# Down products in two operations, and a new order of every engine's work, in a kernel of attention and a gated two-layer product

## The chip, the cores and the metric

The kernel runs on one core of one Trainium2 chip. The metric is the time of one execution in microseconds (us) of device time, lower is better, given as the median of several runs. Beside the runs stands one profiled execution, whose trace gives each engine's instructions and waits.

Engines are called as the profile calls them: PE is TensorE (its products; PEld its weight loads), DVE is VectorE, ACT is ScalarE, POOL is GpSimd, SP is SyncE, whose queue issues every transfer here.

## The reference

Blocked attention with a local window and block summaries over 4 batches, 8 heads, 768 positions and 64 columns of a head, then two matrix products with a gate between, over 3072 tokens of 512 columns and 2048 inner columns:

```python
k_sum = k.reshape(B, H, nb, block, D).max(axis=3)      # nb = 24 blocks of 32
v_sum = v.reshape(B, H, nb, block, D).mean(axis=3)
scores_l = scale * q @ k.T          # where |row - column| < 16, else -1e9
scores_s = scale * q @ k_sum.T + log(block)
a = softmax(concat(scores_l, scores_s))
x = a @ concat(v, v_sum)            # laid out as 3072 x 512
h = x @ w_in                        # w_in 512 x 2048, w_out 2048 x 512
out = (h * cos(h)) @ w_out
```

Inputs q, k and v are float32; the two weight matrices come as float64.

## The kernel before, in words

The tokens are worked in eight blocks of 384 (half a batch each). In each block attention runs in four groups of two heads, called a, b, c and d with the block's number: a0 is the first group of block 0. The two products run in 128 **steps** s0 to s127, one for each block and each of 16 slices of 128 inner columns; block 0 is worked in two parts (slices 0 to 5, then 6 to 15), with block 1 between.

A **step** is this chain (class Step): *up*, 12 products on PE of 128x128 by 128x384 into one PSUM bank (line 707); *turns* on ACT (717), *residue* on DVE (720), *sine* and *square* on ACT (725, 728), *gate* on DVE (732), which together make h * cos(h) with the sign turned; *high part*, the gate's result rounded to a narrower float32 form (a copy, on ACT line 343 or on DVE line 345); *low part*, what the rounding left (a subtraction, line 349, on POOL or DVE); *down*, 9 products of 128x128 by 128x512 into three banks that stay open for all steps of a block (line 754). The products are made exact enough by splitting both sides in high and low: up multiplies x high by w_in high, x low by w_in high and x high by w_in low; down multiplies, for each of three chunks of 128 tokens, gate high by w_out high, gate high by w_out low and gate low by w_out high, in this order. The tiles t, gh and gl of the chain have two buffers each (pool gp), so step n + 2 writes what step n read.

A **group** loads q, k and v, turns q and k (on PE with an identity matrix, lines 495 and 508, or on DVE in squares of 32), makes *scores* (48 small products on 64 rows and 64 columns of PE, line 562) into two banks, *scales* them out of the banks (573, or a copy), subtracts the maximum (POOL), takes the exponential (ACT, line 599, with a table load when the table changes), divides by the sum (POOL), turns the result (*tp* with its copies *cp*, line 619, or through DRAM) and multiplies it with the values (*va*, 24 products on 120 rows and 64 columns, line 663) into one bank, from which x high and x low are taken (343 or 345, 349).

The float64 **weights** w0 to w15 are loaded a slice at a time, 1 MB each in two transfers (lines 364 and 368), and turned into a high and a low float32 part by integer operations: *magnitude* on ACT (line 381), four operations on DVE (386, 392, 400, 408), *high part* (343 or 345) and *low part* (349). The sums of v by blocks (v0_0 and so on) are made on DVE and POOL and spread to the groups by small transfers (line 486).

What sets the order: one table, ORDER, a string of words written out ahead. Each word names who (s5, a2, w3), what (up, hi, dn, and so on), the PSUM banks, and the engine where there is a choice (a for ACT, v for DVE, p for POOL). A loop at the end of the kernel goes through it and issues each word's instructions; every engine keeps that order, and so does SP's queue of transfers. Semaphores make an instruction wait for what it needs; behind a waiting instruction everything later on its engine waits too. Eight PSUM banks are shared by all: three hold the open sums of down, the other five go round among ups, turns, scores and values.

Of the kernel before, what the change touches and what calls it, by code (L numbers as in the profile page):

```python
# [32 lines left out]
d0.sc c0.su w1.lb a0.tp.0.0 w0.ab.1 a0.tp.1.4 d1.q w1.fb.0 a0.cp.0.a w2.l a0.cp.1.a w0.cl d0.z.1.a w1.hi.a w5.l
w0.sh.0.1 a0.va.5 d0.z.0.a b0.m w1.lo.p w0.lb c0.ex d0.m a0.xh.a d0.mx c0.sm d0.su w3.l c0.iv w2.ab.1 a0.xl c0.nm
w0.fb.0 d0.ex b0.v c0.tp.0.6 w2.cl w0.hi.a d0.sm c0.tp.1.7 c0.cp.0.a w0.lo.p c0.m w2.sh.2.3 c0.cp.1.a w2.lb w5.ab.1
c1.q w2.fb.0 a1.q d0.iv w2.hi.a w5.cl d0.nm d0.v w5.sh.4.5 c0.va.0 w4.l w5.lb w3.ab.1 w2.lo.p d1.m d0.tp.0.1 c0.xh.a
b0.mx d0.tp.1.6 c0.xl d0.cp.0.a b0.su a1.tq.7 b1.q w5.fb.0 d0.cp.1.a d0.va.2 a1.cq.a a1.m b0.ex w3.cl a1.ms.3.0
w5.hi.a w3.sh.6.7 d1.v a1.sc d0.xh.a w5.lo.p b0.sm w4.ab.1 c1.tq.1 c1.v c1.ms.4.5 w3.lb a1.z.1.a a1.z.0.a b1.tq.0
b0.iv b1.m w4.cl b0.nm c1.cq.a b1.cq.a a1.mx c1.sc c1.m w4.sh.0.1 c1.z.1.a a1.su b0.tp.0.3 c1.z.0.a b0.tp.1.5 d0.xl
a1.v b0.cp.0.a w4.lb b1.ms.4.2 b0.cp.1.a a1.ex w8.l c1.mx b0.va.3 b1.v a1.sm b1.sc c1.su b0.xh.a b0.xl d1.tq.5  # L40
b1.z.1.a a1.iv s0.up.3 a2.q w4.fb.0 a1.nm c1.ex b1.z.0.a b2.v c1.sm w4.hi.a d1.ms.2.0 c1.iv w3.fb.1 s0.tu c1.nm
d1.cq.a a1.tp.0.1 w7.l w4.lo.v s1.up.4 w3.hi.a w9.l a1.cp.0.a w3.lo.p b1.mx w8.ab.0 w6.l d1.sc s0.re s1.tu w8.cl
a1.tp.1.5 v1_0.l s2.up.6 d1.z.0.a w10.l b1.su d1.z.1.a s1.re a1.cp.1.a s0.si d1.mx a1.va.7 w8.sh.0.1 d1.su a2.tq.2
a2.v c1.tp.0.5 s0.sq w8.lb s1.si s1.sq c1.cp.0.a s0.ga s1.ga c1.tp.1.5 s0.hi.a w8.fb.1 s1.hi.a s0.lo.p c1.cp.1.a
w9.ab.0 s0.dn.3.4.5 s1.lo.p w8.hi.v b2.q s2.tu d1.ex s2.re w8.lo.p a2.cq.v a1.xh.v s3.up.0 a1.xl s2.si d1.sm v1_0.s.p
d1.iv w9.cl c1.va.1 s2.sq d1.nm v1_1.l s3.tu s1.dn c1.xh.a s3.re w7.ab.1 c1.xl s2.ga s2.hi.a w7.cl s4.up.2 s3.si
s2.lo.p w9.sh.6.7 s3.sq b1.ex v1_1.s.p s3.ga d1.tp.0.1 w9.lb d1.tp.1.0 s2.dn s4.tu b1.sm v1_2.l d1.cp.1.a d1.cp.0.a
s4.re s5.up.0 s3.hi.a b1.iv w9.fb.0 b1.nm s4.si w9.hi.v s3.lo.p d1.va.1 w7.sh.6.7 s4.sq d1.xh.a w9.lo.p s3.dn s5.tu
w7.lb w10.ab.1 s5.re s4.ga s5.si v1_2.s.p d1.xl s4.hi.a b1.tp.0.2 w7.fb.0 s5.sq b1.tp.1.1 b1.cp.0.a b1.cp.1.a s4.lo.p
s5.ga w12.l w7.hi.a b1.va.2 s5.hi.v v1_3.l s4.dn w10.cl s5.lo.p b1.xh.a b1.xl w7.lo.p w10.sh.6.7 s6.up.1 w6.ab.1  # L50
w10.lb w10.fb.0 s7.up.0 s6.tu v1_3.s.p s6.re w10.hi.a w6.cl s5.dn s7.tu s6.si w10.lo.p v1_4.l s6.sq b2.m s7.re s8.up.2
s5.ta.0.a s6.ga s5.ta.1.v s6.hi.a s5.st.0 s5.ta.2.a w6.sh.6.7 s5.st.1 s6.lo.p w12.ab.0 s5.st.2 a2.m w6.lb v1_4.s.p
s6.dn.1.3.4 s8.tu s7.si s8.re s7.sq w12.cl s8.si v1_5.l s9.up.5 s8.sq s7.ga s8.ga s7.hi.a w6.fb.1 s8.hi.a s7.lo.p
s7.dn s9.tu s8.lo.p w12.sh.6.7 w11.l w6.hi.a s9.re w6.lo.p w12.lb s9.si s10.up.0 s9.sq s9.ga w12.fb.0 s9.hi.a s8.dn
s10.tu s9.lo.p s10.re w12.hi.a w15.l v1_5.s.v w11.ab.1 w12.lo.p s11.up.2 v1_6.l s10.si w11.cl s10.sq s9.dn s11.tu
s11.re s10.ga s11.si w11.sh.6.7 s10.hi.a s12.up.5 s11.sq s10.lo.p w15.ab.0 w11.lb v1_6.s.p s10.dn s12.tu s11.ga s12.re
s11.hi.a w11.fb.1 s12.si s11.lo.p v1_7.l s13.up.0 s12.sq s12.ga w11.hi.a w13.l w15.cl s12.hi.a w15.sh.6.7 s11.dn
s13.tu s12.lo.p s13.re w11.lo.p w15.lb s13.si s12.dn s13.sq s13.ga w15.fb.0 s13.hi.a s13.lo.p s14.up.2 w13.ab.1
w15.hi.v w13.cl w15.lo.p s13.dn s14.tu v1_7.s.v s14.re a2.k s15.up.5 w13.sh.6.7 s14.si s14.sq s14.ga w13.lb s14.hi.a
s16.up.0 s15.tu s14.lo.p s15.re w13.fb.0 s15.si s14.dn s15.sq s16.tu s15.ga w14.l w13.hi.a s16.re a2.tk.0.2 s15.hi.a  # L60
w13.lo.p a2.tk.1.6 a2.ks.0 a2.ck.0.a s17.up.7 b2.k a2.ck.1.a a2.ks.1 s16.si s16.sq s15.lo.p a2.sc.5.2 s16.ga s16.hi.a
s15.dn s17.tu a2.z.1.v s16.lo.p s17.re w14.ab.1 a2.z.0.v a2.mx s17.si s16.dn s17.sq w14.cl a2.su s17.ga s17.hi.a
w14.sh.6.7 b2.tk.0.0 s18.up.2 b2.ck.0.a s17.lo.p a2.ex w14.lb s17.dn w14.fb.0 s18.tu a2.sm w14.hi.a b2.tk.1.5 s18.re
b2.tq.6 w14.lo.p b2.ck.1.a c2.k s19.up.7 b2.ks.1 s18.si b2.ks.0 c2.q b2.cq.v a2.iv b2.sc.5.0 a2.nm s18.sq s19.tu
s18.ga s20.up.6 s19.re s18.hi.a b2.z.0.v s19.si s18.lo.p b2.z.1.v s19.sq b2.mx a2.tp.0.2 s20.tu a2.tp.1.5 c2.tq.0
a2.cp.0.a s19.ga b2.su s18.dn d2.q c2.cq.v a2.cp.1.a s19.hi.a s20.re b2.ex s19.lo.p c2.tk.0.7 c2.tk.1.2 c2.ks.0 s19.dn
d2.k c2.ks.1 c2.ck.0.a b2.sm c2.ck.1.a s20.si b2.iv s21.up.5 b2.nm s20.sq s20.ga s22.up.0 s21.tu s20.hi.a s21.re
# [850 lines left out]
```

## Time and profile before

| | |
|---|---|
| median of 3 runs | 678.76 us (675.94 to 678.94) |
| profiled execution, its own time | 681.43 us |
| its span, first to last instruction | 679.6 us |
| busy on PE, DVE, ACT, POOL | 645.0, 391.0, 411.4, 294.2 us |
| granted clock of PE, mean | 0.98 |
| up: 1536 products, down: 1152 products | 37% and 38% of the chain that ended last |
| scores, values on that chain | 4% and 4% |

Busy time of PE counts pipelined products, whose modelled lengths overlap, so it says less than the chain of waits, which goes back from the last instruction to what released each. In a row of the chain stand start, length and what ran; in a row of the waits who waited for whom, then the total, the number of times and the longest.

### The profile page before, as it was taken

Reading aid. Unit: us, or ns where it says so; the run is one execution under the profiler, and the core shown is the slowest. Engines: PE = TensorE matmul, PEld = TensorE weight load, DVE = VectorE, ACT = ScalarE, POOL = GpSimd, SP = SyncE. Lnnn points to the kernel's source line nnn. Section 1 sums busy time; section 2 is a strip of 40 time slices with the busy share of each in tenths; the row PEclk is TensorE's granted clock in tenths of the full one; section 3 lists DMA queues with packets and bytes.
Section 4 is the critical chain, followed back from the end, with each engine's and each line's share of the span. In section 5 each row is a group of like instructions: output and inputs, shape, how many; then the busy total and the mean of one; then the engine's idle time right before and its main releaser. Section 6 shows DMA issues by size and latency. Waiting matters only on the chain.

```text
span 679.6 us, 13400 instructions
## 1 busy us (share of the span) xinstructions
PE 645.0 (95%) x5180; PEld 567.2 (83%) x5180; DVE 391.0 (58%) x642; ACT 411.4 (61%) x720; POOL 294.2 (43%) x312
## 2 busy tenths in 40 slices
PE   6449889999999999999999999999999999999997
PEld 5337668988889888889888888898988889899996
DVE  4888688988552367435875764347584663223221
ACT  3566787758775458646666666447666575455443
POOL 3656588646252355432443653424353352222221
PEclk9859889999999999999999999999999999999999
DMA  9896924532232224434454463334254341001001
GB/s 222 251 245 165 295 53 164 191 101 52 64 89 56 81 63 117 117 91 103 89 145 115 94 193 97 88 50 103 80 131 106 76 133 52 23 0 47 1 0 47
DMA packets 158543, 71.17 MB, mean 105 GB/s; under 512 B 129552, under 2 KB 147344, under 8 KB 158480
## 3 DMA queue, kind: packets, MB, share of 16 engines
q1 hardware_dynamic: 158480, 70.32, 39.4%
q8 instruction: 41, 0.67, 0.4%
q14 instruction: 22, 0.18, 0.1%
HBM read 52.99 MB, written 14.94 MB: 100 GB/s over the span
## 4 chain that ended last, share of the span: by engine, by line
PE 84%; DMA 6%; DVE 3%; ACT 2%; POOL 2%; issue 1%; SPq 1%; ACTq 0%; POOLq 0%
PE banks L754 38%; PE banks L707 37%; PE banks L562 4%; PE banks L663 4%; DMA late<-in_moe_w_out_dram 3%; DMA vn<-vs 1%; PE banks L508 1%; DMA vn<-in_v_dram 1%; DMA x<-vs 1%; SPq L486 1%; DVE stage L408 1%; ACT stage L381 0%; POOL late L252 0%; PE banks L619 0%; DVE stage L386 0%
## 5 line engine op out<-in xcount | busy, mean ns | idle before, releaser
L707 PE MATMUL banks<-xh,w 128*128 128x384 f32 x1024 | 282.1, 339 | 0.0
L754 PE MATMUL banks<-w,gh 128*128 128x512 f32 x768 | 244.6, 400 | 0.0
L349 POOL TENSOR_TENSOR gl<-t,gh 128x384 fp32r<-128x384 f32 x123 | 126.0, 1025 | 252.0 <-ACT gh L343 184.9
L707 PEld LDWEIGHTS banks<-xh,w 128*128 128x128 f32 x1024 | 187.2, 188 | 4.8 <-DVE xl L349 0.2
L707 PE MATMUL banks<-xl,w 128*128 128x384 f32 x512 | 171.9, 336 | 0.0
L754 PEld LDWEIGHTS banks<-w,gh 128*128 128x128 f32 x768 | 141.3, 189 | 26.3 <-ACT gh L343 0.5
L754 PE MATMUL banks<-w,gl 128*128 128x512 f32 x384 | 152.7, 398 | 0.8 <-POOL gl L349 0.8
L720 DVE SCALAR_TENSOR_TENSOR t<-t,banks 128x384 f32<-128x384 int32 x128 | 70.3, 549 | 130.3 <-ACT t L717 130.1
L717 ACT ACTIVATE t<-banks 128x384 int32<-128x384 f32 x128 | 62.3, 487 | 104.4 <-PE banks L707 102.7
L732 DVE SCALAR_TENSOR_TENSOR t<-t,banks 128x384 f32<-128x384 f32 x128 | 70.2, 549 | 75.5 <-ACT t L728 75.0
L707 PEld LDWEIGHTS banks<-xl,w 128*128 128x128 f32 x512 | 96.3, 188 | 3.9
L725 ACT ACTIVATE t<-t 128x384 f32<-128x384 f32 x128 | 67.1, 524 | 45.0 <-DVE t L720 44.7
L343 ACT CAST gh<-t 128x384 fp32r<-128x384 f32 x115 | 58.8, 512 | 55.1 <-DVE t L732 50.6
L754 PEld LDWEIGHTS banks<-w,gl 128*128 128x128 f32 x384 | 72.8, 190 | 17.9 <-POOL gl L349 2.1
L728 ACT ACTIVATE t<-t 128x384 f32<-128x384 f32 x128 | 67.2, 525 | 3.7
L586 POOL TENSOR_TENSOR sc<-sc,m 128x720 f32<-128x720 f32 x28 | 40.2, 1437 | 41.7 <-DVE m L581 40.4
L610 POOL TENSOR_TENSOR sc<-sc,r 128x720 f32<-128x720 f32 x28 | 39.1, 1401 | 37.7 <-DVE r L607 35.2
L349 POOL TENSOR_TENSOR w<-stage,w 128x1024 fp32r<-128x1024 f32 x15 | 36.1, 2404 | 16.7 <-ACT w L343 16.0
L562 PEld LDWEIGHTS banks<-kd,qd 64*64 64x64 f32 x1344 | 27.5, 132 | 7.9 <-issue 4.8
L602 DVE TENSOR_REDUCE r<-sc 128x6 f32<-128x726 f32 x28 | 25.2, 902 | 14.2 <-ACT sc L599 14.1
L725 ACT ACT_TABLE_LOAD x24 | 30.8, 1283 | 0.4
L381 ACT ACTIVATE stage<-late 128x1024 f32<-128x1024 f32 x16 | 18.4, 1147 | 20.5 <-DMA late<-in_moe_w_out_dram 18.2
(98 smaller groups left out, 588.8 us busy)
## 6 DMA issues: line engine op xcount, KB each, us to landing
late<-in_moe_w_in_dram SPq DMA_DIRECT2D x16, 512.0 KB
late<-in_moe_w_out_dram SPq DMA_DIRECT2D x16, 512.0 KB
pd<-stage SPq DMA_DIRECT2D x20, 384.0 KB
vn<-in_v_dram SPq DMA_DIRECT2D x52, 120.0 KB
out_dram<-stage SPq DMA_DIRECT2D x23, 256.0 KB
pt<-pd SPq DMA_DIRECT2D x60, 96.0 KB
kn<-in_v_dram SPq DMA_DIRECT2D x24, 192.0 KB
qn<-in_q_dram SPq DMA_DIRECT2D x80, 48.0 KB
```

The lines of the kernel that those rows point to most:

```text
L343: eng.copy(out=out, in_=in_)
L349: eng.tensor_tensor(out=lo, in0=src, in1=hi.bitcast(F32), op=ALU.subtract)
L562: nc.tensor.matmul(out=self.sp[hh][s * QT : (s + 1) * QT, c, lo : lo + n], lhsT=self.qd[rows, t * QT : (t + 1) * QT], rhs=self.kd[rows, ke ...
L586: nc.gpsimd.tensor_tensor(out=self.sc, in0=self.sc, in1=self.m.unsqueeze(2).broadcast_to([P, U, NK]), op=ALU.subtract)
L610: nc.gpsimd.tensor_tensor(out=self.sc, in0=self.sc, in1=self.r.unsqueeze(2).broadcast_to([P, U, NK]), op=ALU.mult)
L707: nc.tensor.matmul(out=self.h, lhsT=w_of(name, self.f)[:, c * P : (c + 1) * P], rhs=x_of(self.blk, part, c), start=n == 0, stop=n == last,)
L717: nc.scalar.activation(out=self.t.bitcast(I32), in_=self.h, func=AF.Copy, scale=1.0 / TWO_PI)
L720: nc.vector.scalar_tensor_tensor(out=self.t, in0=self.t.bitcast(I32), scalar=-TWO_PI, in1=self.h, op0=ALU.mult, op1=ALU.add)
L725: nc.scalar.activation(out=self.t, in_=self.t, func=AF.Sin, scale=0.5)
L728: nc.scalar.activation(out=self.t, in_=self.t, func=AF.Square, scale=math.sqrt(2.0))
L732: nc.vector.scalar_tensor_tensor(out=self.t, in0=self.t, scalar=-1.0, in1=self.h, op0=ALU.add, op1=ALU.mult)
L754: nc.tensor.matmul(out=self.acc[i], lhsT=g[:, i * P : (i + 1) * P], rhs=w_of(name, self.f), start=self.first and n == 0, stop=self.last an ...
```

## The change

**Down in two operations.** The word *dn* goes. *dh* issues the products that use gate high only: six, chunk by chunk, w_out high and then w_out low. *dl* issues the three products of gate low with w_out high. They add into the same three banks; the first *dh* of a block opens them, the last *dl* closes them. In the last step of all (s127) *dh* leaves the third chunk to *dl*, so that its nine products run as they did before.

```diff
-            gh, gl = self.gh, self.gl
-            which = [(i, n) for i in range(NTT) for n in range(3)]
-            if self.g == len(steps) - 1:
-                which[2:5] = [which[3], which[4], which[2]]
+            self.products(self.early())
+
+        def early(self):
+            chunks = range(NTT - 1 if self.g == len(steps) - 1 else NTT)
+            return [(i, n) for i in chunks for n in range(2)]
+
+        def down_low(self):
+            early = self.early()
+            rest = [(i, n) for n in range(3) for i in range(NTT) if (i, n) not in early]
+            self.products(sorted(rest) if len(rest) > NTT else rest)
+
+        def products(self, which):
             for i, n in which:
-                g, name = ((gh, "wo_h"), (gh, "wo_l"), (gl, "wo_h"))[n]
+                g, name = (self.gl if n == 2 else self.gh), ("wo_h", "wo_l", "wo_h")[n]
                 nc.tensor.matmul(
                     out=self.acc[i], lhsT=g[:, i * P : (i + 1) * P], rhs=w_of(name, self.f),
                     start=self.first and n == 0, stop=self.last and n == 2,
...
-            lo="low_part", dn="down", fe="fetch", ad="add", ta="take", st="store",
+            lo="low_part", dh="down", dl="down_low", fe="fetch", ad="add", ta="take", st="store",
```

**A new table.** ORDER is written anew as a whole, by a planner whose costs count each change of PE from one kind of products to another. Every word that it held is there again but for *dn*; the order, the banks and the engines differ. High parts of steps and weights are on DVE 51 times (16 before) and on ACT 93 times (128); low parts on DVE 69 times (6) and on POOL 75 times (138). The line that holds s96's down, before and after:

```diff
-s97.ga c7.su c7.m s98.up.0 s95.ta.0.1.v a7.xh.a b7.sm s95.ta.2.0.a s95.st.0 a7.xl c7.ex s95.st.2 s96.dn.3.4.7 b7.iv
+s96.dh.4.5.7 s97.lo.v b7.po s98.sq c7.sm s99.tu s96.dl s95.ta.1.0.a c7.iv s99.re c7.nm s97.dh s98.ga d7.qt s98.hi.a
```

PE near the end of the program, before: the last products of one up (xl and xh are x low and high of the block), one down whole, and the first products of the next up.

```order
L707 MATMUL banks<-xl_7_6244,w_1532 128x384
L707 MATMUL banks<-xh_7_6236,w_1532 128x384
L754 MATMUL banks<-w_1400,gh 128x512 x2
L754 MATMUL banks<-w_1400,gl 128x512
L754 MATMUL banks<-w_1400,gh 128x512 x2
L754 MATMUL banks<-w_1400,gl 128x512
L754 MATMUL banks<-w_1400,gh 128x512 x2
L754 MATMUL banks<-w_1400,gl 128x512
L707 MATMUL banks<-xh_7_5856,w_1666 128x384
L707 MATMUL banks<-xl_7_5862,w_1666 128x384
```

PE near the end, now: three steps' downs stand together, each as six products of gh and three of gl, with ups on both sides.

```order
L715 MATMUL banks<-xl_7_6184,w_1589 128x384
L715 MATMUL banks<-xh_7_6169,w_1589 128x384
L771 MATMUL banks<-w_1012,gh 128x512 x6
L771 MATMUL banks<-w_1012,gl 128x512 x3
L771 MATMUL banks<-w_1144,gh 128x512 x6
L771 MATMUL banks<-w_1144,gl 128x512 x3
L771 MATMUL banks<-w_1411,gh 128x512 x6
L771 MATMUL banks<-w_1411,gl 128x512 x3
L715 MATMUL banks<-xh_7_5826,w_1665 128x384
L715 MATMUL banks<-xl_7_5887,w_1665 128x384
```

Between the rows of one weight slice and the next there is now no up; the ups stand in runs of two to four, and the products with gl come after all six with gh.

SP's queue at the start, before: late0 from the weights is the load of slice w8; the rows ahead of it are values and summaries of the second block's groups.

```order
L470 DMA late4_129<-in_v_dram 96x5x64 x2
L478 DMA late4_129<-in_v_dram 80x2x64
L470 DMA late4_129<-in_v_dram 96x5x64 x2
L478 DMA late4_129<-in_v_dram 80x2x64
L486 DMA late3_128<-vs0_281 24x6x64 x2
L486 DMA late4_129<-vs1_297 24x6x64 x2
L470 DMA late3_128<-in_v_dram 96x5x64 x2
L478 DMA late3_128<-in_v_dram 80x2x64
L364 DMA late0_125<-in_moe_w_in_dram 128x4x256
L368 DMA late0_125<-in_moe_w_out_dram 128x1024
```

SP's queue at the start, now: the same load of late0.

```order
L478 DMA late4_129<-in_v_dram 96x5x64 x2
L486 DMA late4_129<-in_v_dram 80x2x64
L494 DMA vn1_104<-vs0_281 24x6x64 x2
L478 DMA late3_128<-in_v_dram 96x5x64 x2
L486 DMA late3_128<-in_v_dram 80x2x64
L372 DMA late0_125<-in_moe_w_in_dram 128x4x256
L376 DMA late0_125<-in_moe_w_out_dram 128x1024
L457 DMA qn_138<-in_q_dram 128x3x64 x2
L494 DMA late4_129<-vs1_298 24x6x64 x2
```

The load of w8 has moved up, ahead of summaries and values that came before it, and a query load follows it.

ACT a little later, before: gh are the high parts of s0 and s1, pt the copies of c1's turned exponentials, stage0 from late1 the magnitude of slice w9.

```order
L725 ACTIVATE t_790<-t_790 128x384
L728 ACTIVATE t_790<-t_790 128x384
L343 COPY pt_847<-banks_133 120x512
L343 CAST gh_853<-t_729 128x384
L343 CAST gh_857<-t_790 128x384
L343 COPY pt_847<-banks_133 120x256
L381 ACTIVATE stage0_862<-late1_126 128x1024
L717 ACTIVATE t_880<-banks_133 128x384
```

ACT there, now:

```order
L733 ACTIVATE t_792<-t_792 128x384
L736 ACTIVATE t_727<-t_727 128x384
L736 ACTIVATE t_792<-t_792 128x384
L351 COPY pt_839<-banks_133 120x512
L351 CAST gh_847<-t_727 128x384
L389 ACTIVATE stage0_865<-late1_126 128x1024
L351 CAST gh_883<-t_792 128x384
L725 ACTIVATE t_886<-banks_133 128x384
```

The second copy of pt has left ACT (it is on DVE now), and w9's magnitude stands between the two high parts.

More of the change, by code (lines that the diff above doesn't have):

```diff
@@ L33 @@
[L33 to L67, printed above, removed]
@@ new lines @@
+d0.v w2.fb.1 c0.va.7 d1.m w5.sh.4.5 w2.hi.a d0.tp.0.6 c0.xh.a w2.lo.p b0.mx a0.xh.a a1.tq.0 w4.l w3.ab.0 w5.lb
+d0.tp.1.2 a1.m b1.tq.3 d0.cp.1.a a0.xl b0.su a1.cq.a w5.fb.1 a1.ms.2.1 d0.cp.0.a d1.v b0.ex w3.cl a1.sc w5.hi.a b0.sm
+b0.m d0.va.0 a1.z.0.a c0.xl w5.lo.p c1.tq.6 w3.sh.4.5 d0.xh.a a1.v b1.cq.a a1.z.1.a b0.iv w3.lb w4.ab.0 c1.ms.7.1
+b0.nm w8.l d0.xl c1.cq.a d1.q w4.cl b0.tp.0.0 c1.sc a1.mx c1.m b0.tp.1.6 w4.sh.2.3 a1.su c1.z.1.a c1.z.0.a c1.v
+b0.cp.1.a b1.ms.1.7 c1.mx b0.cp.0.a w4.lb c1.su a1.ex b0.va.6 w7.l b1.sc a1.sm b0.xh.a b1.m b0.xl d1.tq.0 b1.z.0.a
@@ new lines @@
+s14.dh s15.sq s16.tu s15.ga w14.l s14.dl s16.re a2.tk.0.3 s15.hi.v s16.si a2.tk.1.6 s17.up.7 s16.sq a2.ks.1 b2.k
+a2.ck.0.a s15.lo.v a2.ck.1.a a2.ks.0 s16.ga a2.sc.2.6 w13.hi.v s17.tu s16.hi.a s17.re b2.tq.3 s18.up.5 a2.z.0.v
+a2.z.1.v w14.ab.1 s16.lo.v a2.mx s17.si s15.dh s17.sq w14.cl a2.su s17.ga s15.dl w14.sh.6.7 s17.hi.a s16.dh s17.lo.p
+a2.ex w14.lb w13.lo.p s16.dl s17.dh w14.fb.1 s18.tu b2.cq.a b2.tk.0.2 w14.hi.a b2.tk.1.6 s19.up.7 b2.ks.1 c2.k
+b2.ck.0.a w14.lo.p s18.re b2.ck.1.a c2.q b2.ks.0 s18.si a2.sm b2.sc.3.6 a2.iv a2.nm s19.tu s20.up.2 b2.z.0.v s18.sq
@@ new lines @@
+v3_3.s.v s68.si b5.pi s68.sq s67.lo.p s66.dl s68.ga s70.up.7 s69.tu s68.hi.a s69.re v3_4.l s68.lo.v s69.si d5.ex
+s71.up.5 s69.sq d5.sm b5.va.2 s70.tu a5.xh.a s67.dh c5.pi b5.xh.a b5.xl a6.qt s67.dl d5.iv s68.dh s70.re d5.nm d5.m
+s69.ga s70.si s69.hi.v s68.dl d5.v s69.lo.v s69.dh d5.pt.1 s71.tu s70.sq s71.re c5.va.2 d5.po s70.ga s71.si s69.dl
+v3_4.s.v s70.hi.a s71.sq s72.up.6 v3_5.l s71.ga a5.xl s70.lo.v s73.up.7 s72.tu s72.re s72.si v3_5.s.v s71.hi.a
+s74.up.5 s71.lo.p v3_6.l d5.pi s73.tu s72.sq s70.dh s72.ga s73.re s75.up.4 s72.hi.a c5.xh.v s73.si s70.dl s71.dh
@@ new lines @@
+s101.hi.v s102.si d7.sm s101.lo.p s101.dh d7.iv d7.nm c7.pi s101.dl s102.sq s103.tu s102.ga s104.up.3 s103.re d7.pt.0
+s103.si s103.sq d7.po s105.up.2 s103.ga s102.hi.v s103.hi.v s102.lo.p c7.va.1 s104.tu s103.lo.p s102.dh s104.re
+s104.si d7.pi s105.tu s102.dl c7.xh.a s103.dh s104.sq s104.ga s104.hi.v s103.dl c7.xl s104.dh s105.re s104.lo.v
+s105.si s105.sq s104.dl s105.ga d7.va.0 s105.hi.a s106.up.6 s107.up.3 s106.tu d7.xh.a d7.xl s106.re s108.up.1
+s105.lo.v s107.tu s107.re s109.up.2 s107.si s107.sq s106.si s107.ga s106.sq s110.up.0 s106.ga s106.hi.a s106.lo.v
@@ new lines @@
+s118.dh s119.hi.v s119.lo.v s120.ga s121.tu s118.dl s121.re s119.dh s121.si s120.hi.a s120.lo.v s119.dl s122.tu
+s120.dh s121.sq s122.re s121.ga s122.si s120.dl s122.sq s123.up.0 s122.ga s121.hi.v s122.hi.v s121.lo.p s124.up.2
+s123.tu s123.re s122.lo.v s125.up.4 s124.tu s123.si s124.re s124.si s124.sq s121.dh s123.sq s123.ga s121.dl s123.hi.a
+s122.dh s123.lo.v s124.ga s125.tu s122.dl s124.hi.v s125.re s123.dh s124.lo.v s125.si s125.sq s123.dl s125.ga
+s126.up.3 s125.hi.v s127.up.6 s126.tu s126.re s125.lo.v s124.dh s127.tu s126.si s127.re s126.sq s124.dl s126.ga
@@ L170 @@
+s125.dh s126.hi.a s127.si s126.lo.p s125.dl s127.sq s126.dh s127.ga s127.hi.v s127.lo.p s126.dl s127.dh s127.dl
+s127.ta.1.0.a s127.ta.0.1.v s127.ta.2.a s127.st.1 s127.st.2 s127.st.0
 """
```

228 lines of the change are left out of this document (122 added, 106 removed).

## The prediction

> **What bounds the kernel now.** I read the page first, then who waited for whom on TensorE, then the busy times of the last stage. The page gives the span and TensorE's share; the second fence is the waits of TensorE from 103 us on (total, times, longest), the third the last stage (its bounds and length, then busy time and instructions by engine, TensorE's granted clock, DMA share, GB/s).
>
> ```profile
> span 679.6 us, 13400 instructions
> PE 645.0 (95%) x5180; PEld 567.2 (83%) x5180; DVE 391.0 (58%) x642; ACT 411.4 (61%) x720; POOL 294.2 (43%) x312
> ```
> ```profile
> PE banks L754 <- POOL gl L349: 0.4, 1, 0.4
> ```
> ```profile
> 165.00:680.00 515.00, 510.38 (x3966) 454.87 (x3960) 257.78 (x470) 303.08 (x538) 192.16 (x200) 1.00 0.32 81
> ```
>
> From 103 us to the end TensorE waits 0.4 us in all, at full clock, while no other engine is busy for 60% of the last stage. So behind 103 us only TensorE's own time counts: how long its products take and how they follow each other. Before 103 us it waits for loads and other engines. The sum has these two halves.
>
> **What one change of kind costs.** The chain of waits late in the program (start, length, line; 12 products are one up, 9 one down):
>
> ```profile
> 600.22 2.10 PE banks L707 x12
> 602.33 2.08 PE banks L754 x9
> ...
> 629.53 2.10 PE banks L707 x12
> 631.63 4.12 PE banks L754 x18
> 635.75 4.18 PE banks L707 x24
> 639.94 2.08 PE banks L754 x9
> ```
>
> From 600.22 to 629.53 seven rounds of one up and one down pass: 29.31 / 7 = 4.187 us each, 8.374 for two. From 631.63 to 639.94 the same work runs as two downs and two ups: 8.31. One round of changes (up to down and back) costs 0.064 us. It is small and in every round.
>
> The other kind of change is to attention's products, which use 64 rows or columns of the array (the line of values here):
>
> ```profile
> 579.39 2.11 PE banks L707 x12
> 581.50 0.85 PE banks L663 x24
> 582.35 2.26 PE banks L754 x9
> ```
>
> Up, values and down end at 582.35 + 2.26 = 584.61 and take 5.22 us; a round without the visit takes 4.187 and the values 0.85, so going in and out costs 0.18.
>
> **The change, part by part.** *Ups and downs.* The number of products is the same: the split gives 6 and 3 instead of 9, no weight load and no bank is added. I counted, in the old and the new table, TensorE's operations from the fifth up (s4) to the end, about where TensorE stops waiting. Up to down goes from 77 to 38, down to up from 88 to 41: (39 + 47) / 2 = 43 rounds at 0.064 = **-2.8 us**. Nothing hides this; TensorE has no idle time there to give it back to. Whether the step from a step's high products to its low ones has a price is shown by no row: within a down every third product is a low one already and 18 in a row take 4.12, so I take nothing; the other end is half a round, 0.03, for 128 steps, 3.8 us lost.
>
> *Visits to attention.* Going in falls from 41 to 35, coming out from 41 to 36, since more scores and values stand side by side: 5.5 x 0.18 = **-1.0**. The Trainium skill (TensorEngine Tiling (Array Packing), section Tiling Modes, Key Properties) says that changing the tiling mode, not merely the tile, drains TensorE; by that rule alone the sum would hold this term and not the one before.
>
> *The low part's wait.* The only wait behind 103 us is a down that stood at its third product for the low part:
>
> ```profile
> 146.76 0.50 PE L754 MATMUL banks<-w,gl 128*128 128x512 f32 x1 [0.42 <-POOL gl L349]
> ```
>
> With the low products behind all six high ones, that wait has 0.9 us more cover: **-0.4**.
>
> *Start.* Waits of TensorE from 45 to 103 us, and the two waits of ACT that stand behind the first of them, with the load's issue:
>
> ```profile
> PE banks L663 <- DMA x<-vs: 7.6, 1, 7.6
> PE banks L619 <- ACT pt L343: 2.5, 1, 2.5
> PE banks L619 <- DVE t L732: 1.5, 1, 1.5
> PE banks L663 <- ACT pt L343: 0.8, 1, 0.8
> ```
> ```profile
> 68.50 1.13 ACT L381 ACTIVATE stage<-late 128x1024 f32<-128x1024 f32 x1 [2.75 <-DMA late<-in_moe_w_out_dram]
> 79.22 1.14 ACT L381 ACTIVATE stage<-late 128x1024 f32<-128x1024 f32 x1 [3.31 <-DMA late<-in_moe_w_out_dram]
> ```
> ```profile
> 18.74 2.44 SPq L470 DMA_DIRECT2D x<-in_v_dram  x2
> ...
> 31.25 1.64 SPq L486 DMA_DIRECT2D vn<-vs  x2
> ...
> 35.22 0.49 SPq L368 DMA_DIRECT2D late<-in_moe_w_out_dram  x1
> 37.48 2.63 SPq L470 DMA_DIRECT2D vn<-in_v_dram  x2
> ```
> ```profile
> 21.77 4.64 DMA vn<-in_v_dram
> 40.69 4.09 DMA x<-vs
> ```
> ```profile
> 82.70 0.73 PE L754 MATMUL banks<-w,gh 128*128 128x512 f32 x2
> ```
>
> The first row of ACT is the magnitude of slice w8, the second that of w9. ACT, in order, waits 2.75 us for w8 with s1's turns, c1's copies and s0's sines queued behind it; so TensorE's 2.5. In the new order w8's load stands five rows earlier in SP's queue, at 0.5 to 2.6 us a row. The 0.8 (b1's values behind their copy) gets s4's high products between, about 1.4 us, and the 1.5 (a transpose into the bank of s3's up) gets 7.6 us of TensorE's work instead of 5.3 in front.
>
> Against that: c0's values load goes from 18.74 (the first row of SP above) to behind c0's summaries, which went out at 40.69, landed 4.09 later and were what TensorE waited 7.6 us for. Ahead of the summaries there lack now w3's load with SP's idle time behind it (1.1 + 1.8), b0's summaries (1.6, at 31.25) and c0's own old place (2.9), and there is one query load more (two DMAs, about 0.5 each as at 35.22): they go out near 34, c0's values till 39, and with a landing of 4.6, which the neighbouring load of values took from 21.77, arrive near 43, against 44.8. And w9's 3.31 us on ACT now stand in front of s1's high part, ready then near 79.22 + 1.14 + 0.51 = 80.9; its down ran at 82.70, so that is free. Bounds: all of 2.5 + 1.5 + 0.8 and 2 us of the 7.6 gained is -6.8; a landing 4 us later than that estimate and nothing else gained is about +3. I take **-2.0**, below the middle of the gains, since the waits form a chain and one that goes uncovers the next.
>
> *New waits.* Durations from the groups of instructions (count, busy, mean ns, idle before):
>
> ```profile
> L573 DVE SCALAR_TENSOR_TENSOR sc<-banks,mask 128x360 f32<-128x360 f32 x48 | 23.4, 522 | 10.2 <-PE banks L562 10.1
> L343 ACT CAST gh<-t 128x384 fp32r<-128x384 f32 x115 | 58.8, 512 | 55.1 <-DVE t L732 50.6 <-PE banks L754 3.0 <-PE banks L663 0.7
> L345 DVE CAST gh<-t 128x384 fp32r<-128x384 f32 x13 | 5.4, 415 | 1.5 <-DVE t L732 0.5
> L349 POOL TENSOR_TENSOR gl<-t,gh 128x384 fp32r<-128x384 f32 x123 | 126.0, 1025 | 252.0 <-ACT gh L343 184.9 <-issue 37.6 <-DVE gh L345 10.9
> L349 DVE TENSOR_TENSOR gl<-t,gh 128x384 fp32r<-128x384 f32 x5 | 2.9, 583 | 2.0 <-ACT gh L343 1.9
> L599 ACT ACT_TABLE_LOAD x23 | 29.5, 1283 | 0.4
> L599 ACT ACTIVATE sc<-sc 128x720 f32<-128x720 f32 x28 | 22.3, 805 | 3.4 <-POOL sc L586 3.1
> ```
>
> Three times (c4, b7, d3) an up takes a bank of scores with only one group's values, 0.85 us, between; the scale that empties it takes 0.52 when VectorE is free. A busy VectorE costs up to 0.6 there: I take 0.3 for all three. The high part has two buffers. In 26 places of the new table the downs of three steps stand together, and the third's high part can be written only when the first's high products are done: between lie 0.68 + 1.37 + 0.68 = 2.7 us, the write takes 0.51, the low part then 1.03 on POOL, with 4.1 us to its use. Behind the waiting write on ACT stand later steps' turns, but their ups come only after these downs. Covered, so nothing; without cover it is the rival below. The moves among engines (high parts on VectorE 16 to 51, low parts 6 to 69) add 35 x 0.415 + 63 x 0.583 = 51 us to VectorE's 391 in a span of 680: no bound. **+0.3** in all.
>
> The sum: -2.8 - 1.0 - 0.4 - 2.0 + 0.3 = **-5.9 us**. The profiled execution took 681.43 us, 2.7 above the median of the three runs; the terms are differences, so I take them from the median: 678.76 - 5.9 = **672.9**.
>
> **The rivals.**
> *The wait for the high part's buffer (slower).* If ACT is in an exponential with its table loads when a high part becomes writable, it is late by 1.28 + 0.81 + 1.28 = 3.4 us, against 2.2 of slack: 1.2 us of TensorE. On VectorE the same write can stand behind POOL; the trace shows one operation at two lengths:
>
> ```profile
> 48.73 0.69 DVE L386 TENSOR_SCALAR stage<-stage 128x1024 f32<-128x1024 f32 x1
> 53.67 1.52 DVE L386 TENSOR_SCALAR stage<-stage 128x1024 f32<-128x1024 f32 x1 [0.89 <-ACT stage L381]
> ```
>
> The Trainium skill (SBUF — State Buffer, Terms) calls the port pair that VectorE and GpSimd share an exclusive lock, held for a whole instruction; the 1.52 agrees. It speaks against moving work to VectorE while POOL keeps half of the low parts. The price is (26 places) x (lateness): it decides from 9.3 / 26 = 0.36 us at each, where the gain of 5.9 turns to a loss of 3.4. One late by 1.2 us in every two gives 15.6 - 5.9: 688. For it: two buffers and long runs of downs. Against it: from the end of an up to its down's start lie 8 us in the middle now and 13 after, and the old order's tightest places caused 0.4 us. Chance 0.11.
>
> *Only the array's mode costs.* If the 0.064 of a round is not a price of the change but backlog that longer runs pay elsewhere, the first term goes: 675.7, no change. This is what the skill's rule on draining would give. Two ups at 4.18 against 2.10 each speak against it. Chance 0.08.
>
> *The start gives it back.* c0's values land 4 us later and the rest isn't gained: +3 instead of -2, 677.9. For it: TensorE's longest wait hangs on just these loads, and SP's queue is strict. Chance 0.13.
>
> *The start gives more.* All its bounds: -6.8 instead of -2, 668.1. For it: most of these waits hang on ACT standing behind two loads, and one of the two comes earlier. Chance 0.15.
>
> **How the numbers follow.** The forecast itself (671 to 675) has 0.53. A measurement here can tell about 0.5%, 3.4 us, from no change: faster is below 675.4. That holds the forecast and the larger gain, 0.68; the two middle rivals are no change, 0.21; slower 0.11. The range leaves out the slower rival and the far end of the larger gain: 666.5 to 679.5.
>
> **What would show it.** Right: behind 103 us TensorE's waits stay under 1 us; two ups still take 4.18 and a round's price is unchanged; the last stage is shorter by about 3.5 us for the same work. The start: TensorE's 2.5 and 0.8 are gone and c0's values run at about 45 or before. Wrong: TensorE's weight loads waiting for gh or gl, or products waiting for DVE's scale, by more than 3 us; the step from high to low products costing 0.03 each; or TensorE's last wait of the start coming after 103.

## The result and the profile after

The kernel after takes 666.31 us (median of 4, 665.60 to 667.27), the kernel before 677.53 (median of 4, 675.94 to 678.94): ratio 0.9836, 95% interval 0.9805 to 0.9867. It is faster by 11.2 us. The forecast was 5.9 faster, 672.9 us, with a range down to 666.5: the direction was right, the size about half. A second timing of the same kernel (e5 below) gave 667.30 where before took 676.27, 9.0 us less.

The first lines of the page of the kernel after (span, TensorE and its weight loads, then the other engines):

```profile
span 664.6 us, 13329 instructions
PE 638.3 (96%) x5180; PEld 565.8 (85%) x5180; DVE 444.7 (67%) x772; ACT 372.3 (56%) x664; POOL 215.8 (32%) x218
```

The 5180 products are the same. VectorE took over 54 us of work and reached 67%: no bound, as was said. From 103 us to the end the view of TensorE's waits has no row at all now (before: one, of 0.4 us). The chain of waits late in the program (start, length, line; an up is 12 products in line 715, a whole down 9 in line 771):

```profile
600.31 6.26 PE banks L715 x36
606.57 6.16 PE banks L771 x27
612.73 6.26 PE banks L715 x36
619.00 4.12 PE banks L771 x18
623.12 4.18 PE banks L715 x24
627.30 8.20 PE banks L771 x36
635.51 6.26 PE banks L715 x36
```

Ups and downs stand in threes; two ups still take 4.18, three downs 6.16, or 2.053 each against 2.08 for one between two ups. The last stage:

```profile
165.00:664.60 499.60, 495.32 (x3899) 443.91 (x3897) 305.63 (x577) 260.43 (x473) 114.25 (x105) 1.00 0.32 83
```

It holds 67 products fewer than the 515.00 us quoted of before, since the start ended earlier. So I compare by work instead of by time. From the start times of all products I took the pace of each kind when its own kind stands ahead of it (an up 2.080 us, a down 2.040, scores 0.888, values 0.705, three transposes 0.33): the whole program is 600.8 us of TensorE at that pace. What a profiled execution takes beyond this, from the start of its span to TensorE's last product, I call **lost time**. Before lost 49.99 us ahead of 103 us and 24.17 behind it; after lost 40.62 and 18.49. The profiled execution of before took 681.43 us, though, more than any of the 35 executions of that kernel that were timed beside the last four runs below (672.97 to 680.63). So the 5.7 us behind 103 us can be trusted at once, the 9.4 of the start can't. Medians leave 11.2 - 5.7 = 5.5 for the start.

TensorE's four longest waits of the start, 45 to 103 us, after, and two magnitudes on ScalarE (w8's and w9's), with the second DMA of five slices' loads on SP (w8, w7, w9, w6, w10):

```profile
PE banks L627 <- POOL sc L618: 1.3, 1, 1.3
PE banks L557 <- ACT pt L351: 1.0, 1, 1.0
PE banks L570 <- ACT qd L509: 0.7, 1, 0.7
PE banks L503 <- ACT pt L351: 0.5, 1, 0.5
```
```profile
63.16 1.16 ACT L389 ACTIVATE stage<-late 128x1024 f32<-128x1024 f32 x1
72.14 1.18 ACT L389 ACTIVATE stage<-late 128x1024 f32<-128x1024 f32 x1 [0.42 <-POOL late L594]
```
```profile
53.72 0.35 SPq L376 DMA_DIRECT2D late<-in_moe_w_out_dram  x1
59.84 0.51 SPq L376 DMA_DIRECT2D late<-in_moe_w_out_dram  x1
66.54 0.51 SPq L376 DMA_DIRECT2D late<-in_moe_w_out_dram  x1
67.58 1.23 SPq L376 DMA_DIRECT2D late<-in_moe_w_out_dram  x1
69.52 0.46 SPq L376 DMA_DIRECT2D late<-in_moe_w_out_dram  x1
```

w8's magnitude, which stood 2.75 us, waits for nothing; w9's, which stood 3.31, stands 0.42. The view names POOL for that, but the trace has the end of w9's load at 72.06, and in every run here a magnitude that waits for its load starts 0.07 to 0.11 us after that end: the 0.42 is still for the load. TensorE's 2.5, 1.5 and 0.8 are gone. c0's values:

```profile
39.67 1.55 PE L671 MATMUL banks<-pt,x 120*64 120x64 f32 x24 [3.78 <-DMA x<-in_v_dram]
```

They run at 39.67 instead of 44.92. Yet the up of s0 begins at 59.75, against 60.87: what those values gained was given back before it.

### The profile page after: what moved, and what is told of

It is laid out like the page before. It is cut to its first block, busy times and chain, and to the rows that moved or that the text cites. A ratio compares the mean times of both kernels' runs of the same rounds, so it can differ in the third digit from the quotient of the medians.

```text
span 664.6 us, 13329 instructions
## 1 busy us (share of the span) xinstructions
PE 638.3 (96%) x5180; PEld 565.8 (85%) x5180; DVE 444.7 (67%) x772; ACT 372.3 (56%) x664; POOL 215.8 (32%) x218
## 4 chain that ended last, share of the span: by engine, by line
PE 89%; DMA 4%; SPq 3%; DVE 2%; issue 1%; ACT 1%
PE banks L715 40%; PE banks L771 40%; PE banks L570 4%; PE banks L671 3%; DMA late<-in_moe_w_out_dram 2%; SPq L457 1%; DMA qn<-in_q_dram 1%; SPq L494 1%; PE banks L627 1%; DMA late<-in_q_dram 1%; DVE banks L400 1%; PE banks L516 0%; PE banks L503 0%; DVE banks L408 0%; DMA vn<-vs 0%
## 5 line engine op out<-in xcount | busy, mean ns | idle before, releaser
L715 PE MATMUL banks<-xh,w 128*128 128x384 f32 x1024 | 273.0, 337 | 0.0
L771 PE MATMUL banks<-w,gh 128*128 128x512 f32 x768 | 198.6, 394 | 0.0
L357 POOL TENSOR_TENSOR gl<-t,gh 128x384 fp32r<-128x384 f32 x60 | 61.2, 1021 | 242.6 <-ACT gh L351 80.1
L771 PE MATMUL banks<-w,gl 128*128 128x512 f32 x384 | 109.8, 393 | 0.0
L733 ACT ACTIVATE t<-t 128x384 f32<-128x384 f32 x128 | 66.4, 523 | 46.3 <-DVE t L728 46.0
L771 PEld LDWEIGHTS banks<-w,gl 128*128 128x128 f32 x384 | 71.2, 188 | 14.4
L736 ACT ACTIVATE t<-t 128x384 f32<-128x384 f32 x128 | 65.9, 521 | 2.1
L351 ACT CAST gh<-t 128x384 fp32r<-128x384 f32 x81 | 41.4, 511 | 43.3 <-DVE t L740 26.2
L618 POOL TENSOR_TENSOR sc<-sc,r 128x720 f32<-128x720 f32 x28 | 39.5, 1412 | 51.1 <-DVE r L615 43.2
L357 DVE TENSOR_TENSOR gl<-t,gh 128x384 fp32r<-128x384 f32 x68 | 40.7, 598 | 18.3 <-PE banks L771 9.7
L581 DVE SCALAR_TENSOR_TENSOR sc<-banks,mask 128x360 f32<-128x360 f32 x48 | 24.1, 524 | 14.2 <-PE banks L570 14.1
L570 PE MATMUL banks<-kd,qd 64*64 64x96 f32 (+1 forms) x1344 | 31.6, 234 | 0.7 <-ACT qd L509 0.7
```

Source lines behind the costliest of these rows:

```text
L351: eng.copy(out=out, in_=in_)
L357: eng.tensor_tensor(out=lo, in0=src, in1=hi.bitcast(F32), op=ALU.subtract)
L570: nc.tensor.matmul(out=self.sp[hh][s * QT : (s + 1) * QT, c, lo : lo + n], lhsT=self.qd[rows, t * QT : (t + 1) * QT], rhs=self.kd[rows, ke ...
L618: nc.gpsimd.tensor_tensor(out=self.sc, in0=self.sc, in1=self.r.unsqueeze(2).broadcast_to([P, U, NK]), op=ALU.mult)
L715: nc.tensor.matmul(out=self.h, lhsT=w_of(name, self.f)[:, c * P : (c + 1) * P], rhs=x_of(self.blk, part, c), start=n == 0, stop=n == last,)
L733: nc.scalar.activation(out=self.t, in_=self.t, func=AF.Sin, scale=0.5)
```

## The experiments

All kernels are the reference's computation in full. "Split" stands for downs in two operations, "the start" for the words up to the up of s6, about the first 358. An edit of the order is shown by the words that move. The theory: half of the gain is in the start and hangs on the slices' loads, half is in TensorE's order behind it, and the split is a detail. The rivals: the start's share is the accident of one slow profile; or the split is what carries it.

| kernel | median, us | ratio (95% interval) | profiled, us | lost before 103 | lost behind 103 |
|---|---|---|---|---|---|
| before | 677.53 | | 681.43 | 49.99 | 24.17 |
| after | 666.31 | 0.9836 (0.9805 to 0.9867) | 666.54 | 40.62 | 18.49 |
| e1 split only | 676.55 | 1.0002 (0.9976 to 1.0027) | 674.12 | 44.02 | 22.83 |
| e2 start new | 672.65 | 0.9926 (0.9900 to 0.9952) | 672.67 | 42.00 | 23.37 |
| e3 rest new | 672.39 | 0.9931 (0.9906 to 0.9956) | 672.64 | 46.50 | 18.55 |
| e4 no split | 673.51 | 0.9956 (0.9933 to 0.9979) | 673.09 | 42.87 | 22.95 |
| e5 after again | 667.30 | 0.9861 (0.9834 to 0.9888) | 667.08 | 41.14 | 18.42 |
| e6 old, three loads early | 676.35 | 0.9994 (0.9978 to 1.0009) | 676.70 | 45.95 | 23.47 |
| e7 new, w8 late | 675.13 | 0.9972 (0.9949 to 0.9994) | 676.81 | 50.71 | 18.75 |
| e8 new, c0 early | 667.45 | 0.9866 (0.9846 to 0.9885) | 667.12 | 41.14 | 18.45 |
| e9 old work, new loads | 672.67 | 0.9941 (0.9921 to 0.9961) | 672.58 | 42.52 | 22.77 |
| e10 new work, old loads | 672.33 | 0.9924 (0.9901 to 0.9948) | 672.88 | 47.02 | 18.55 |
| e11 old, w8 moved | 673.28 | 0.9940 (0.9918 to 0.9962) | 675.44 | 45.38 | 22.79 |
| e12 old, w8 and w7 moved | 676.82 | 0.9989 (0.9969 to 1.0008) | 674.18 | 43.79 | 23.10 |
| e13 old, w8 and w9 early | 674.83 | 0.9965 (0.9946 to 0.9985) | 674.81 | 44.70 | 22.85 |
| e14 new queue, w9 late | 675.47 | 0.9980 (0.9957 to 1.0004) | 673.90 | 43.79 | 22.80 |
| e15 split only again | 676.54 | 0.9983 (0.9962 to 1.0003) | 676.75 | 46.64 | 22.83 |
| e16 w8 moved again | 676.07 | 0.9995 (0.9972 to 1.0018) | 673.62 | 43.56 | 22.78 |

### Halves of the change: e1 to e5

**e1**: the old order, split.

```diff
-s6.dn.1.3.4
+s6.dh.1.3.4 s6.dl
```

> The old order, with each down written as its six high products and directly behind them its three low ones; nothing else is changed. Theory (the order carries the gain, the split little): what goes is the 0.4 us wait for a low part and some smaller ones, and the step from an up to a down gets cheaper by about 0.01 us at some 80 places: 1 to 1.5 us under the kernel before, about 676. Rival (the step from high to low products costs 0.03 us, 128 times): 3.8 us above it, about 681.

The step from high to low products costs nothing: the low ones take 0.680 us behind the high ones' 1.360. Behind 103 us 1.3 us went. That is the theory's size, but not its sum: s14's down had lost 0.81 of them, with the 0.42 wait, and s6's 0.28, while the cheaper step at some 80 places is not there (a down between two ups takes 2.08 us either way). The view of waits has no row there now. In the median nothing of it shows, nor in e15; 1.3 lies inside both intervals. The rival's 3.8 us is refuted.

**e2** and **e3**: one order up to the up of s6, the other behind it (e2's cut; e3 is the counterpart).

```diff
 ... s5.dh b1.xl w10.lb
-s6.up.5 s5.lo.p w6.ab.0 w10.fb.1
+b2.v a2.v s5.lo.p s6.up.5 w6.ab.1 w10.fb.0
 ...
```

> The new order up to the up of s6 (358 words, about the first 95 to 103 us), and from there all that is left in the old order (bank numbers renamed, downs split). Theory (half of the gain is made in the start): 1.3 us for the split as in the run with the split alone, and 5.5 to 9.5 us for the start: 667 to 671. Rival (the start gives the 2.0 us of the prediction, and the profiled execution of the kernel before had a slow start by chance): 674 to 675.

> The counterpart: the old order up to the up of s6, then what is left in the new order (bank numbers renamed). Theory: the rest of the program gives 5 to 6 us, split included: 671.5 to 672.5. Rival (the start gives only 2.0): the rest carries 9 us, 668 to 669.

Against e1 the new start brings 3.9 us (672.65), the new rest 4.2 (672.39), so e3 is as the theory had it and e2 lies between the two. The start gives about twice the 2.0 of the forecast, and the 9.4 of the two profiles was in part an accident, as the rival said. Behind 103 us the new order lost 18.4 to 18.8 us in all six kernels that have it with the split, the old one 22.8 to 23.5 in all ten that have it so: about 4.4 us between them, in every execution.

**e4**: the new order, whole downs at the place of the low products.

```diff
-s7.dh ... s7.dl
+... s7.dn
```

> The new order with whole downs as before (nine products, chunk by chunk, each chunk's low one third), at the place of the low products. Theory (downs stand in runs, so a low part is late at few of them: 4 places, 0.9 us, worked out from the ends of the low parts in the trace of the kernel after, and 0.5 us for a dearer step from up to down): 1.4 us above the kernel after, about 668. Rival (the split is what lets the downs run together; every run's first down now waits for its low part): 5 us and more above the kernel after, 672 or later, with TensorE's waits on gl in the trace.

The time is the rival's: 673.51, 6 to 7 us over the kernel after. Behind 103 us 22.95 us are lost, 4.4 more than with the split, and ahead of it 1.7 to 2.2 more. TensorE's waits there:

```profile
PE banks L751 <- DVE gl L346: 1.5, 1, 1.5
PE banks L704 <- DVE sc L570: 1.1, 2, 0.7
PE banks L704 <- POOL w L346: 0.5, 1, 0.5
```

One down waits for its low part in a run of downs, two ups for a bank of scores, one for a weight: the waits that the forecast looked for in the kernel after are here. They are 3.1 of the 4.4 us. The rival's mechanism, that every run's first down waits for its low part, isn't there: one does. So the split is worth 1.3 us in the old order (24.17 to 22.83) and 4.4 in the new (22.95 to 18.49), and the order 1.2 without the split and 4.3 with it. My theory that the split is a detail is wrong. Whole downs were run at this one place alone; what an order planned for whole downs would give is not shown.

**e5**: after, unchanged.

> The kernel after, unchanged, for a median beside the kernel before on this chip and for a second profile. Theory (the rest of the program gives 5.7 us in every execution, the start 4 to 6 on the mean of executions): 665.5 to 668, TensorE's time beyond its products after 103 us 18.5 again. Rival (the first ratio was luck): above 669.

667.30: as expected; the gain is no luck of four executions.

**A round's price**, from the traces of e1 and after. Behind the last values e1 has 32 changes between ups and downs and lost 1.378 us, after has 13 and lost 0.734: (1.378 - 0.734) / 9.5 rounds = 0.068 us. The same place in e1:

```profile
601.29 2.10 PE banks L712 x12
603.40 2.08 PE banks L768 x9
605.48 2.10 PE banks L712 x12
607.58 2.08 PE banks L768 x9
```

### The start: e6 to e16

TensorE's order in the start is the same in before, e1, e6, e9 and e11 to e16, so the time from the up of s0 to that of s6, the **stretch**, can be compared among them: 42.5 (before), 38.6 (e1), 39.5 (e15, e1's kernel again). In the kernel after it is 35.5, in e5 35.2, with the high products of s5's down in it, 1.4 us that come later in the old order.

**e6**: three loads of the old queue moved forward.

```diff
-... b0.cp.1.a a1.ex w8.l
+... w2.lo.p w8.l ... w5.lo.p w7.l ... w3.fb.1 w9.l
```

> The old order with downs split, and three of SP's words moved forward: the load of slice w8 by 10 words of SP's queue (behind w4's), that of w7 by 8, and that of w9 by one (to stand right behind the word that frees its buffer). Theory (the start's gain comes from slices that land too late in the old order; ScalarE's waits on them were 10.9, 5.7 and 1.7 us in three executions of the old start): those waits go, the median falls by 2 to 3 us against the run with the split alone (676.55), to about 674, and the runs scatter less. Rival (one wait that goes uncovers the next, as the prediction had it): 676 or more, with the waits on other rows.

Both were half right. No magnitude waits for a load, and the stretch is 36.2 us. But the up of s0 begins at 63.00, against 58.68 in e1: for b1's queries, now behind w8, TensorE waits 2.3 us, where e1 has no such wait. Nothing is left in the median.

**e7**: w8's load behind a2's queries.

```diff
-a1.v w8.l d1.q c1.m c1.v
+a1.v d1.q c1.m c1.v
 ...
-a2.q w9.l
+a2.q w8.l w9.l
```

> The new order with one word moved back: the load of w8 behind the query load of a2, 8 words of SP's queue later, which issues it at about 62 us as in the kernel before instead of 52.8. Theory: w8's magnitude, which starts at 63.2 us without a wait, waits about 5 us for it, and TensorE loses 2 to 4 us: 668.5 to 670.5. Rival (the new start has slack for it, its gain is in the order of TensorE's work): within 0.7 us of the kernel after.

More than expected: 7.8 us over e5. SP was busy in front of it, and the load's second DMA went out at 68.28. ScalarE's wait for it, and TensorE's behind that:

```profile
68.28 0.50 SPq L373 DMA_DIRECT2D late<-in_moe_w_out_dram  x1
```
```profile
73.25 1.12 ACT L386 ACTIVATE stage<-late 128x1024 f32<-128x1024 f32 x1 [10.60 <-DMA late<-in_moe_w_out_dram]
```
```profile
PE banks L668 <- ACT pt L348: 9.4, 1, 9.4
```

This is the forecast's chain (ScalarE stands at a magnitude, the copies behind it are late, TensorE waits for them), four times as long.

**e8**: c0's summaries and values forward in the new order.

```diff
-w2.l b0.v w5.l d0.m b1.q c0.m c0.v
+w2.l c0.m c0.v w5.l d0.m b1.q
 ...
-d0.v d1.m
+d0.v b0.v d1.m
```

> The new order with the loads of c0's summaries and values ahead of w5's (five words forward) and b0's values behind d0's. Theory (TensorE's longest wait left, 3.8 us of c0's values at 36 to 40 us, hangs on SP's queue alone): that wait falls under 1 us and 1.5 to 3 us of it stay gained: 663.5 to 665. Rival (the next thing, the transposes behind POOL's normalisation, is late by as much): 666 to 667.

The rival's time was right. c0's values run 0.75 us earlier than in the profile of the kernel after and the up of s0 0.77, but then s2's down and d1's transposes take it back, and 667.45 is e5's time. Behind that stands w9's load; its magnitude in e8:

```profile
72.71 1.13 ACT L386 ACTIVATE stage<-late 128x1024 f32<-128x1024 f32 x1 [1.78 <-POOL gl L354]
```

The load ends at 72.64, so this wait too, which the view gives to POOL, is for the load. ScalarE comes to the magnitude 0.8 us earlier than in the kernel after and starts it 0.6 us later. From there its work follows 0.5 us late, and with it the high part that s2's down waits for and POOL's normalisation ahead of the transposes.

**e9** and **e10**: SP's queue in the one order, the other four engines in the other, in the start alone.

```diff
 SP, first words from v0_1.l on:
-b0.q w1.l d0.q w0.l c0.v a0.v a0.m d1.q w2.l w5.l
+b0.q w1.l d0.q w0.l a1.q a0.v a0.m w2.l b0.v w5.l
 ...
```

> The old order with downs split, but in the first 359 words (to the up of s6) SP's queue issues its loads in the new order; the other four engines keep the old one. Theory (the start's gain is SP's order): 4 to 5 us under the run with the split alone, about 672. Rival (work and loads have to fit each other; neither order alone gains): 675.5 to 678, or later, with new waits of ScalarE and VectorE on loads.

> The counterpart: the new order, but SP's queue in the first 358 words as in the old one. Theory (SP's order): the start's gain goes, 4 to 5 us above the kernel after, about 672. Rival (fit): the moved load of w8 alone cost 7.8 us; with the whole old queue at least 4 us, up to 9: 671 to 676, with ScalarE waiting on w8 again. A third way (the order of TensorE's, ScalarE's and VectorE's work carries the gain, and only w8's place matters on SP): the gap to the kernel after is at most w8's part, and the other run stays at 676.

The medians are the theory's: SP's queue carries the start's gain. The new queue under the old work brings 3.9 us against e1, just what the whole new start brought in e2; the old queue under the new work costs 5.0 against e5. In e9 c0's values run at 39.90, but the up of s0 at 59.61: given back, as in the kernel after. Its stretch is 36.2. In e10 no slice is late, against the rival, which had ScalarE waiting for w8: c0's values run at 44.98 again, TensorE waits another 4.3 us for b1's queries, and the up of s0 begins at 66.65. So slices are not all that the queue decides.

**e11, e12**: which rows of the queue.

```diff
-d1.v c1.v b1.m c1.m a1.v w8.l
+d1.v w8.l c1.v b1.m c1.m a1.v
```

and in e12 also

```diff
-b2.v w7.l
+c1.m w7.l ... b2.v
```

> The old order with downs split, and one word of SP's queue moved: the load of w8 by five rows, from behind a1's values to right behind d1's (the place it has in the new order); no query load is pushed back. In the run with three loads early, TensorE's stretch from the up of s0 to that of s6 took 36.2 us instead of 38.6 to 42.5, but b1's queries, now behind w8, came 2 us late ahead of it. Theory (late slices are what the old start loses): the up of s0 starts where it did, at 58.7 to 60.9, the stretch falls under 38.6, the median by 1 to 3 us against 676.55: 673.5 to 675.5. Rival (the gain needs the whole new queue): within 1 us of 676.55.

> As the run beside it, and w7's load too, from behind b2's values to behind c1's summaries, so that w9's, w6's and w10's loads stand one row nearer. Theory: the stretch from the up of s0 to that of s6 falls to about 36.2 us, the value it has in both runs in which no slice was waited for; median 672 to 674. Rival: within 1 us of 676.55.

The medians contradict each other: e11's (673.28) is its theory's, e12's (676.82) its rival's. The profiles are alike: w8's wait is gone in both, w9's is there, 2.17 us in e11 and 1.77 in e12. In e11:

```profile
64.04 1.18 ACT L386 ACTIVATE stage<-late 128x1024 f32<-128x1024 f32 x1
74.57 1.14 ACT L386 ACTIVATE stage<-late 128x1024 f32<-128x1024 f32 x1 [2.17 <-DMA late<-in_moe_w_out_dram]
```

The stretch stays at 39.4 and 39.0. In e12 w7's load is out of the way, 9 us ahead of w9's; but w9's goes out only at 67.83, 3.4 us before ScalarE comes to its magnitude. Four more runs follow.

**e13**: w8's load as in e11, and w9's ahead of w7's and b2's values. **e14**: e9 with the reverse.

```diff
 e13
-a2.q b2.v w7.l w9.l
+a2.q w9.l w7.l b2.v
```
```diff
 e14
-w7.l b1.m v1_0.l b1.v a2.q w9.l
+b1.m v1_0.l b1.v a2.q b2.v w7.l w9.l
```

> The old order with downs split; w8's load right behind d1's values, and w9's directly behind a2's queries, ahead of w7's and of b2's values (the place it has in the new queue). Theory (the old start loses its time to two late slices, w8 and then w9, whose wait comes up once w8's is gone): no magnitude waits for a load any more, the stretch from the up of s0 to that of s6 falls from 39 to about 36.2 us; the profiled run's time lost before 103 us falls to 41.5 to 43.5, the median to 672 to 674. Rival (it takes the whole new queue, c0's values too): the stretch stays at 38 or more.

> The kernel with the old work and the new queue (672.67), but with b2's values and w7's load put back ahead of w9's. Theory: w9's magnitude waits 2 us again and the stretch grows from 36.2 to about 39 us; median 674.5 to 676. Rival: within 1 us of 672.67, stretch 36 to 37.

**e15** and **e16** repeat e1 and e11.

> The run with the split alone once more, as it is, beside the two above: median 675.5 to 677.5, the stretch anywhere from 38.5 to 42.5 us. Rival (its first profile was typical): a stretch of 38.6 again.

> The run with w8's load alone moved, as it is. Its median lay 3.3 us under the split alone, while its profile showed w9's magnitude waiting 2.2 us and a stretch of 39.4 us. Theory (w9's wait takes over, as in the run with w7's load moved too): 675 to 676.5 on the mean of both. Rival (w8 alone is worth 3 us): 672.5 to 674 again.

w9's magnitude in e13, e14, e9 and e16, in this order:

```profile
73.20 1.18 ACT L386 ACTIVATE stage<-late 128x1024 f32<-128x1024 f32 x1
```
```profile
73.07 1.15 ACT L386 ACTIVATE stage<-late 128x1024 f32<-128x1024 f32 x1 [1.42 <-DMA late<-in_moe_w_out_dram]
```
```profile
72.67 1.17 ACT L386 ACTIVATE stage<-late 128x1024 f32<-128x1024 f32 x1
```
```profile
73.74 1.14 ACT L386 ACTIVATE stage<-late 128x1024 f32<-128x1024 f32 x1 [0.72 <-DMA late<-in_moe_w_out_dram]
```

e14 is as the theory said: with b2's values and w7's load back ahead of w9's the stretch is 38.6 instead of 36.2, the median 2.8 us higher (675.47). e13 is half of it: no wait for either load, a stretch of 37.9 and 1.7 us under e15, but the median, the stretch and the lost time (44.70) all miss the theory's figures. e16 doesn't repeat e11's 3.3 us: 676.07, and 674.7 on the mean of both, just under the theory's 675; its stretch is 37.0, 2.4 less than e11's for the same kernel.

The ten traces with the old work, put in the order of what ScalarE waits for w8 and w9 together, show what late slices do. (In e1 and e15 w8's wait of 1.24 us is counted; the view gives it to VectorE, but the load ends 0.1 us before the magnitude begins.)

| run | wait for w8 and w9, us | stretch, us |
|---|---|---|
| e6, e9, e13 | 0, 0, 0 | 36.2, 36.2, 37.9 |
| e16, e14, e12 | 0.7, 1.4, 1.8 | 37.0, 38.6, 39.0 |
| e11, e15, e1 | 2.2, 2.4, 2.5 | 39.4, 39.5, 38.6 |
| before | 6.1 | 42.5 |

So the stretch grows with the wait, by about 1 us for each us of it. That is a tendency, from one trace a run: e13 without a wait is longer than e16 with one. What one row of the queue is worth in the median is less sure. w8 alone gives 1.9 us on the mean of its two runs, w8 and w9 together 1.7, w7 and b2's values away from in front of w9 2.8 with the rest of the new queue in place; each is no more than the 2.8 us by which two timings of one kernel differ (e11 and e16). The whole queue's 3.9 stands clear of e1, and barely of e15 (intervals to 0.9961 and from 0.9962). Which other rows make up the rest stays open. So does 1 to 2 us between the sum of the parts (e1 less 3.9 less 4.2 is 668.5) and the kernel after (666.3 and 667.3).

Why w9 was late in e14: its load's second DMA goes out 0.95 us later than in e9, and w7's just ahead of it.

```profile
64.58 0.50 SPq L373 DMA_DIRECT2D late<-in_moe_w_out_dram  x1
65.61 0.95 SPq L373 DMA_DIRECT2D late<-in_moe_w_out_dram  x1
```
```profile
58.67 0.48 SPq L373 DMA_DIRECT2D late<-in_moe_w_out_dram  x1
64.66 0.50 SPq L373 DMA_DIRECT2D late<-in_moe_w_out_dram  x1
```

The first fence is e14 (w7, w9), the second e9. In e14 w9's load ends at 72.99, 7.4 us after its issue, in e9 at 70.73, 6.1 us after. Of the 2.26 us between them 0.95 is the later issue and 1.31 the longer landing. The rows that counted were put in just ahead of the late load.

## Why the prediction was right or wrong, by its own steps

**What bounds the kernel.** Right. Behind 103 us TensorE's own time is all there is, and it fell without any other engine becoming a bound.

**Ups and downs, -2.8.** Right: 0.068 us a round where 0.064 was read, and -2.6 to -2.9 us by the traces of e1 and after, by how a place between this kind of change and the next is counted; the two together are -4.3.

**Visits to attention, -1.0.** Right in kind, too small: -1.3 to -1.7 us by the same count. Going in costs 0.095 and coming out 0.131 us, 0.226 together; the 0.18 came from one row in which a change of ups and downs, saved by the visit, was set against it.

**High to low products, free.** Right: 0.680 us for the low ones.

**The low part's wait, -0.4.** Too small, and the wrong question. In the old order the split gave 1.3 us: s14's down alone had lost 0.81, of which the view of waits names 0.42. And the new order without the split has waits of 3 us of its own, at the place that e4 gives the whole downs, and the split takes them away. I priced the split in the old order and the order as if it were split, each against before; neither number holds for the pair.

**New waits, +0.3.** None came. With whole downs at the place of the low products two such waits on scores come up, 1.1 us in all (e4), so this too goes with the split.

Together the part behind 103 us was forecast at -3.9 and is -5.7.

**The start, -2.0: the step that failed.** "I take -2.0, below the middle of the gains, since the waits form a chain and one that goes uncovers the next." The step is the term that was mis-sized: the new start brings 3.9 us against e1 (e2), SP's new queue alone the same 3.9 (e9), and the first pair of medians leaves 5.5. Two of its readings failed. c0's values were reckoned to come near 43 us and ran at 39.67, yet all of that was given back before the up of s0, so they are not the gain. And the step left w9's 3.31 us standing, in front of a high part that has time for it; in the new order that wait is 0.42 (0.11 in e5, 0.94 in e2). w7's load goes out 6.7 us ahead of w9's instead of 2.0, and e14, which puts it back close ahead, has 1.42 us of the wait and 2.4 of the stretch again. The forecast priced w8's new place in SP's queue and not what went away from in front of w9's.

The reason given for taking less, that one wait that goes uncovers the next, is only in part borne out. c0's values show it. For the slices the runs don't: with w8 in time w9's magnitude waited 2.17, 1.77 and 0.72 us (e11, e12, e16), with w8 late 3.31, 1.22 and 1.11 (before, e1, e15). How much of the 3.9 is w9's and how much other rows' stays open.

Behind it stands a second fault. The waits were priced from one execution, and none of the kernel before that was timed later is as slow. ScalarE's waits for slices in it (total, times, longest; 38 to 104 us):

```profile
ACT stage L381 <- DMA late<-in_moe_w_out_dram: 10.9, 5, 3.3
```

and in e1, with the same queue:

```profile
ACT stage L386 <- DMA late<-in_moe_w_out_dram: 1.7, 2, 1.2
```

With w8's 1.24, which the view gives to VectorE, that is 2.9. A price of a wait that hangs on landing times needs more than one execution.

**The rivals.** The slower one (the high part's buffer, VectorE behind POOL) didn't come: no product waits behind 103 us, and the view of weight loads names a gh for 0.7 us in all, none of it on a down. That only the array's mode costs is refuted by the round's 0.068 us. That the start gives it back holds for c0's values alone. That the start gives more, 668.1 us with a chance of 0.15, is nearest to what came: 3.9 to 5.5 us, between the forecast's 2.0 and this rival's 6.8. With 1.8 us more behind 103 us as well, the time lies 0.2 us under a range that ended at 666.5; e5's 667.30 for the same kernel lies inside it, so on which side of the end it fell is chance, and the mis-sized start is not.
